# Three of the outer sums of the up product by accumulating DMA, in a two-level Strassen kernel

## The chip, the cores and the metric

The kernel runs on one core of one Trainium2 chip. The metric is the device time of one execution in microseconds (us). A core has five engines that run side by side and meet only at semaphores: PE (TensorE, matrix products), DVE (VectorE) and POOL (GpSimd) for elementwise work, ACT (ScalarE, here copies, scalings and relu), and SP (SyncE, which here only begins transfers). The transfers themselves run on 16 DMA engines that all queues share. In the profile "PEld" is PE's loading of weights, which overlaps its products.

## The reference

Attention without softmax, normalised per head, feeds a mixture of four experts; each token's output is the sum of all four, weighted by given probabilities.

```python
# q, k, v: (8, 8, 576, 64); w1: (4, 512, 1024); w2: (4, 1024, 512); probabilities: (4608, 4)
kv = np.einsum('bhsd,bhse->bhde', k, v)
o = np.einsum('bhsd,bhde->bhse', q, kv)
o = o / np.sqrt(np.mean(o * o, axis=-1, keepdims=True) + 1e-06) * g_norm
x = o.transpose(0, 2, 1, 3).reshape(4608, 512)
p = domain_probs / (domain_probs.sum(-1, keepdims=True) + 1e-09)
for e in range(4):
    h = np.maximum(x @ w1[e], 0.0)           # "up"
    out += p[:, e:e + 1] * (h @ w2[e])       # "down"
```

Everything is float32, inputs and outputs.

## The kernel before

The kernel cuts the 4608 tokens into nine chunks of 512 and works through 36 steps, `s = e * 9 + c`, one for each expert `e` and chunk `c`. A step is an up product (512 tokens by 512 by 1024), relu, and a down product (512 by 1024 by 512).

Both are computed with Strassen's scheme in the Winograd form: seven products of blocks of half the size in place of eight, and more sums. In the up product it is applied twice. The outer level has seven products `m` in the order `OUTER`; each is formed from seven inner products `mm` in the order `ORDER`, whose 128x256 results leave PSUM through ACT copies and DVE additions into one SBUF tile of 128x1024, `made[m]`. The outer sums then combine these seven tiles into the hidden blocks `h[1]`, `h[21]`, `h[4]`, `h[2]` (after relu) and the four differences `h[7]`, `h[5]`, `h[6]`, `h[3]` that the down product needs:

```python
ORDER = (1, 6, 2, 5, 7, 4, 3)
OUTER = (1, 2, 6, 5, 3, 7, 4)
...
def up(s, e, views):
    ...
    def add(key, to, a, b, op=ALU.add, where=either):      # one 128x1024 sum, on DVE or POOL
        combine(key, where(2 * NT), lambda: to.ap[:], lambda: a.ap[:], lambda: b.ap[:], op, [a, b], [to])

    def relu(key, b):
        plan.add(key, act(2 * NT), lambda eng: nc.scalar.activation(
            out=b.ap[:], in_=b.ap[:], func=ACT.Relu), reads=[b], writes=[b])

    for i, m in enumerate(OUTER):
        whole = made[m] = Buf("big", f"m{n}")
        ...                                                 # the seven inner products and their copies
        key = s + (i + 1) / 7
        def unit(f):
            h[f] = Buf("big", f"h{f}_{s}")
            return h[f]
        if m == 2:
            add(key, unit(1), made[1], made[2])
            relu(key, h[1])
        elif m == 6:
            add(key, made[1], made[1], made[6])
        elif m == 5:
            add(key, made[6], made[1], made[5])
        elif m == 3:
            add(key, unit(21), made[6], made[3])
            relu(key, h[21])
            add(key, unit(7), h[1], h[21], ALU.subtract)
        elif m == 7:
            add(key, made[1], made[1], made[7])
            add(key, unit(4), made[1], made[5], where=dve)
            relu(key, h[4])
            add(key, unit(5), h[21], h[4], where=dve)
            add(key, unit(6), h[5], h[1], ALU.subtract, dve)
        elif m == 4:
            add(key, unit(2), made[1], made[4])
            relu(key, h[2])
            add(key, unit(3), h[2], h[6], ALU.subtract)
```

No instruction is written in its final order. Each call of `plan.add` records an operation with the engines that may run it and an assumed cost; `Plan.layout` then plays the program through against those assumptions, and what it settles (which engine, in what order, in which buffer) is the program. So a change of one operation moves many others. The assumptions that matter here are these. In-order engines execute exactly this list, so where a transfer takes longer than assumed, the engine that comes to its result waits, and all that stands behind it waits too.

```python
CROSS, SAME, LANES = 0.3, 0.06, 8             # us from an end to a start on another, the same engine
...
op.end = busy[eng] = t + op.cost[eng]
if op.kb:
    op.end += 5.5                             # a transfer begun on POOL: 5.5 us after its issue
...
def either(n):
    return {"DVE": 0.155 + 0.00104 * n, "POOL": 0.15 + 0.00225 * n}
```

The down product of most steps of the later three experts (`down_deep`) has two levels as well; its inner sums run on DVE or POOL as well. Step 0 uses no Strassen in its up product, and the down products of expert 0 and of each expert's last chunk have one level (`down`). PSUM has eight banks: `u1` and `u2` (two each) for the up products, `db` and `ab` (two each) for the down products and attention. The very last step, 35, is a `down` with nothing after it:

```python
def down(s, e, c):
    ...
    for t in range(2):
        banks = {}
        for j, m in enumerate(MERGED):        # (1, 6, 5, 7, 4, 3, 2)
            kind = "ab" if e and t else "db"
            if m == 1:
                banks[1] = Buf(kind, f"d1_{s}_{t}")
            elif m in (2, 5):
                banks[2] = Buf("u2" if s == E * NCH - 1 else kind, f"d{m}_{s}_{t}")
            ps = banks[1 if m in (1, 6, 7, 4) else 2]
```

The weighted results of the later experts are added to the output in DRAM by transfers begun on POOL with `accum_op=ALU.add` (`send`, line 1065); expert 0 stores plainly from SP. The inputs of each step's up product are loaded again from DRAM by SP into five `xf` buffers.

Of the kernel before, what the change touches and what calls it, by code (L numbers as in the profile page):

```python
# [10 lines left out]
ALU = mybir.AluOpType  # L11
# [23 lines left out]
class Plan:  # L35
# [20 lines left out]
    def add(self, key, cost, fn, reads=(), writes=(), parts=(), kb=0, after=(), port=False, holds=()):  # L56


        op = Op(key, cost, fn, reads, list(writes) + list(parts), kb, port)
        for o in after:  # L60
            op.deps[o] = True
        for b in reads:
            for w in b.writers:
                op.deps[w] = True
            b.readers.append(op)
        for b in writes:
            for o in b.writers + b.readers:
                if o is not op:
                    op.deps[o] = True
            b.readers, b.writers = [], [op]  # L70
        for b in parts:
            b.writers.append(op)
        for b in holds:
            b.readers.append(op)
            op.bufs.append(b)
        for b in op.bufs:
            b.left += 1
        self.ops.append(op)
        return op
# [151 lines left out]
def kernel(  # L231
# [36 lines left out]
    nc = tc.nc  # L268

    B, H, S, D = q.shape  # L270
    E, DM, F = moe_w1.shape
# [5 lines left out]
    NCH = B + 1  # L277
# [56 lines left out]
    plan = Plan()  # L334
# [7 lines left out]
    def act(n):  # L342
        return {"ACT": 0.155 + 0.00088 * n}
# [507 lines left out]
    def up(s, e, views):  # L851
        made = {}
        h = {}

        def add(key, to, a, b, op=ALU.add, where=either):
            combine(
                key, where(2 * NT), lambda: to.ap[:], lambda: a.ap[:], lambda: b.ap[:], op,
                [a, b], [to],
            )

        def relu(key, b):
            plan.add(
                key, act(2 * NT),
                lambda eng: nc.scalar.activation(out=b.ap[:], in_=b.ap[:], func=ACT.Relu),  # L864
                reads=[b], writes=[b],
            )

        for i, m in enumerate(OUTER):
            n = f"{s}_{m}"
            whole = made[m] = Buf("big", f"m{n}")  # L870
            bank = {
                1: Buf("u1", f"u1_{n}"), 2: Buf("u2", f"u2_{n}"), 5: Buf("u2", f"u3_{n}"),
            }
            snap = {}
            for j, mm in enumerate(ORDER):
                key = s + (i + j / 7) / 7
                ps = bank[{2: 2, 5: 5, 3: 5}.get(mm, 1)]

                def product(eng, m=m, mm=mm, ps=ps):
                    for u in range(2):  # L880
                        nc.tensor.matmul(  # L881
                            ps.ap[:, u * P:(u + 1) * P],
                            lhsT=w1f[e][m][mm][1]()[:, u * P:(u + 1) * P], rhs=views[m][mm][1](),
                            start=(mm in (1, 5) and u == 0), stop=True, skip_group_check=True,
                        )

                op = plan.add(
                    key, pe(2, P), product,
                    reads=w1f[e][m][mm][0] + [views[m][mm][0]] + ([ps] if mm == 2 else []),
                    **{"parts" if mm == 2 else "writes": [ps]},  # L890
                    after=last[-2:-1] if mm == 1 else seeds if mm == 5 else (),
                )
                op.marks, op.seed = (ps, HN), mm == 2
                if mm == 3:
                    last.append(op)

                def copy(to, where, ps=ps, key=key):
                    return plan.add(
                        key - 0.4, act(HN),
                        lambda eng: nc.scalar.activation(  # L900
                            out=where(), in_=ps.ap[:, 0:HN], func=ACT.Copy),
                        reads=[ps], parts=[to],
                    )

                def total(a, t, src, add_, whole=whole, key=key):
                    plan.add(
                        key - 0.4, dve(HN),
                        lambda eng: nc.vector.tensor_tensor(  # L908
                            out=block(whole, a, t), in0=src.ap[:, 0:HN], in1=add_.ap[:], op=ALU.add),
                        reads=[src, add_], parts=[whole],  # L910
                    )

                if mm == 1:
                    seeds = [copy(bank[2], lambda b=bank[2]: b.ap[:, 0:HN])]
                elif mm in (6, 7):
                    snap[mm] = Buf("snap", f"s{mm}_{n}")
                    copy(snap[mm], lambda b=snap[mm]: b.ap[:])
                if mm == 2:
                    copy(whole, lambda whole=whole: block(whole, 0, 0))
                elif mm == 7:  # L920
                    total(1, 1, bank[5], snap[7])
                elif mm == 4:
                    copy(whole, lambda whole=whole: block(whole, 1, 0))
                elif mm == 3:
                    total(0, 1, ps, snap[6])
            key = s + (i + 1) / 7

            def unit(f):
                h[f] = Buf("big", f"h{f}_{s}")
                return h[f]  # L930

            if m == 2:
                add(key, unit(1), made[1], made[2])
                relu(key, h[1])
            elif m == 6:
                add(key, made[1], made[1], made[6])
            elif m == 5:
                add(key, made[6], made[1], made[5])
            elif m == 3:
                add(key, unit(21), made[6], made[3])  # L940
# [6 lines that stand above are left out]
                add(key, unit(5), h[21], h[4], where=dve)  # L947
                add(key, unit(6), h[5], h[1], ALU.subtract, dve)
            elif m == 4:
                add(key, unit(2), made[1], made[4])  # L950
                relu(key, h[2])
                add(key, unit(3), h[2], h[6], ALU.subtract)
        hidden[s] = h
# [123 lines left out]
    def down(s, e, c):  # L1077
        h = hidden.pop(s)
        base = s + 1.2
        merge, send = result(s, e, c, base)  # L1080
        second = []
        for t in range(2):
            banks = {}
            for j, m in enumerate(MERGED):
                key = base + (7 * t + j + 0.5) / 14
                kind = "ab" if e and t else "db"
                if m == 1:
                    banks[1] = Buf(kind, f"d1_{s}_{t}")
                elif m in (2, 5):
                    banks[2] = Buf("u2" if s == E * NCH - 1 else kind, f"d{m}_{s}_{t}")  # L1090
                ps = banks[1 if m in (1, 6, 7, 4) else 2]

                def product(eng, m=m, t=t, ps=ps):
                    for kt in range(4):
                        nc.tensor.matmul(  # L1095
                            ps.ap[:, 0:HN], lhsT=four(h[m])[:, kt // 2, t, kt % 2, :],
                            rhs=w2f[e][m].ap[:, kt * HN:(kt + 1) * HN],
                            start=(m in (1, 2, 5) and kt == 0), stop=(kt == 3),
                            skip_group_check=True,
                        )  # L1100

                op = plan.add(
                    key, pe(4, HN), product, reads=[h[m], w2f[e][m]], writes=[ps],
                    after=second[-1:] if t and m in (1, 5) else (),
                )
                op.marks = ps, HN
                if m == 2:
                    second.append(op)
                i, half, fresh = {
                    1: (t, 0, True), 2: (t, 0, False), 6: (t, 1, True), 3: (t, 1, False),  # L1110
                    5: (2 + t, 1, True), 7: (2 + t, 1, False), 4: (2 + t, 0, True),
                }[m]
                merge(key - 0.4, [ps], lambda ps=ps: ps.ap[:, 0:HN], i, half, fresh)
            send(base + 0.5 * (t + 1), t)
            send(base + 0.5 * (t + 1), 2 + t)
# [171 lines left out]
    for e in range(E):  # L1287
        for c in range(NCH):
            s = e * NCH + c
# [14 lines left out]
            if e and c < NCH - 1:  # L1304
                if not primed:
                    banks = [Buf("ab", f"prime{i}") for i in range(2)]
# [20 lines left out]
    with tc.manual_schedule(engines={ENG.PE, ENG.DVE, ENG.Activation, ENG.Pool, ENG.SP}):  # L1327
# [4 lines left out]
        for op in order:  # L1332
# [6 lines left out]
            made = op.fn(op.eng)  # L1339
# [34 lines left out]
```

## Time and profile before

| | |
|---|---|
| time, median of 3 runs | 1730.51 us (1729.95 to 1730.74) |
| span of the profiled execution | 1728.2 us |
| DVE busy | 1224.7 us, 71% |
| ACT busy | 939.3 us, 54% |
| POOL busy | 614.8 us, 36% |
| DMA: SP's queue (q1) / POOL's queue (q0), share of 16 engines | 35.5% / 10.8% |
| accumulating stores, 256 KB, from issue to landing | 5.7 us median |

Busy time is the time in which an engine has an instruction in flight; begun transfers are not counted for the engine that begins them. The share of a queue is the time that its packets took, divided by 16 engines times the span. A group of instructions is named by the line of the kernel, the engine and "out<-in" in the program's names; line 360 is the helper that records every sum, line 864 the relu, line 881 the up product's matrix instructions, lines 1095 and 1170 those of the one-level and the two-level down product, lines 900 and 1198 the ACT copies out of PSUM, line 1065 the accumulating stores. Each float32 product shows as two matrix instructions.

### The profile page before, as it was taken

The numbers are of one execution on the slowest core, as the hardware profiler recorded it, in microseconds if no ns is written. First come the engines' busy times: TensorE is split into PE (matmuls) and PEld (weight loads), VectorE is DVE, ScalarE is ACT, GpSimd is POOL, SyncE is SP. The second block draws the span as 40 slices with busy tenths as digits, with TensorE's granted clock in tenths as the row PEclk, the third lists the DMA queues.
The fourth block names the chain that finished last, engine by engine and source line by source line (L and its number), as shares of the span: only waits on it lengthen the run. The fifth ranks groups of instructions, "written<-read, shape, count | busy, mean of one in ns | idle before, by whom it ended". The sixth has DMA issues, their size and how long they took to land.

```text
span 1728.2 us, 38444 instructions
## 1 busy us (share of the span) xinstructions
PE 1718.7 (99%) x15334; PEld 1651.4 (96%) x15334; DVE 1224.7 (71%) x1969; ACT 939.3 (54%) x2300; POOL 614.8 (36%) x560
## 2 busy tenths in 40 slices
PE   9999999999999999999999999999999999999998
PEld 7699999999999999999999999999999999999998
DVE  4755655565676777777788877777788877777774
ACT  3454544554444565656555556566655566565652
POOL 2421323133334333333345333333345433333331
PEclk9999999999999999999999999999999999999999
DMA  9756444633433353444464344444475344444442
GB/s 236 224 159 193 154 120 131 193 135 128 147 129 100 93 115 103 115 107 113 131 186 110 99 110 111 111 111 110 109 208 112 98 111 111 111 111 103 114 102 49
DMA packets 148596, 220.94 MB, mean 128 GB/s; under 512 B 49600, under 2 KB 90816, under 8 KB 148416
## 3 DMA queue, kind: packets, MB, share of 16 engines
q1 hardware_dynamic: 133312, 191.21, 35.5%
q0 software_dynamic: 15104, 27.27, 10.8%
q8 instruction: 120, 1.97, 0.5%
q14 instruction: 60, 0.49, 0.1%
HBM read 145.30 MB, written 73.14 MB: 126 GB/s over the span
## 4 chain that ended last, share of the span: by engine, by line
PE 99%; POOL 1%; DVE 0%; ACT 0%; issue 0%; POOLq 0%
PE u L881 45%; PE db L1170 19%; PE db L1095 14%; PE ab L1170 12%; PE ab L1095 2%; PE u L968 2%; PE ab L634 1%; PE ab L1323 1%; PE ab L620 1%; PE ab L678 1%; PE ab L660 1%; PE u L1095 1%; POOL rt L551 0%; PE db L660 0%; PE ab L722 0%; PE ab L704 0%
## 5 line engine op out<-in xcount | busy, mean ns | idle before, releaser
L360 DVE TENSOR_TENSOR big<-big,big 128x1024 f32<-128x1024 f32 (+1 forms) x450 | 442.5, 997 | 36.0 <-ACT big L864 23.8
L881 PE MATMUL u<-xf,big 128*128 128x128 f32 x3104 | 453.0, 275 | 0.0
L881 PEld LDWEIGHTS u<-xf,big 128*128 128x128 f32 x3104 | 401.3, 192 | 2.2
L881 PE MATMUL u<-xf,w1y 128*128 128x128 f32 x2652 | 389.6, 275 | 0.0
L908 DVE TENSOR_TENSOR big<-u,snap 128x256 f32<-128x256 f32 x430 | 181.5, 422 | 235.1 <-PE u L881 175.7
L881 PEld LDWEIGHTS u<-xf,w1y 128*128 128x128 f32 x2652 | 343.4, 192 | 2.2
L900 ACT ACTIVATE snap<-u 128x256 f32<-128x256 f32 x490 | 188.1, 384 | 251.3 <-PE u L881 213.9
L1095 PE MATMUL db<-big,big 128*128 128x256 f32 x1120 | 264.1, 380 | 2.1 <-DVE big L560 2.1
L1095 PEld LDWEIGHTS db<-big,big 128*128 128x128 f32 x1120 | 202.9, 190 | 24.6 <-DVE big L560 2.3
L900 ACT ACTIVATE big<-u 128x256 f32<-128x256 f32 x430 | 165.0, 384 | 110.4 <-PE u L881 74.3
L360 POOL TENSOR_TENSOR big<-big,big 128x256 f32<-128x256 f32 (+1 forms) x138 | 170.2, 1241 | 131.6 <-DVE big L360 44.1
L1170 PE MATMUL db<-big,big 128*128 128x128 f32 x1056 | 146.7, 275 | 0.0
L864 ACT ACTIVATE big<-big 128x1024 f32<-128x1024 f32 x128 | 134.4, 1050 | 2.6 <-POOL big L360 1.3
L1170 PEld LDWEIGHTS db<-big,big 128*128 128x128 f32 x1056 | 132.1, 192 | 0.1
L1236 POOL TENSOR_TENSOR big<-big 128x512 f32<-128x512 f32 x26 | 32.9, 1266 | 269.2 <-DVE big L360 263.9
L1198 ACT ACTIVATE snap<-db 128x256 f32<-128x256 f32 x192 | 68.5, 357 | 99.8 <-PE db L1170 94.9
L360 POOL TENSOR_TENSOR big<-big 128x512 f32<-128x512 f32 (+1 forms) x57 | 70.7, 1240 | 126.9 <-DVE big L360 102.6
L1170 PE MATMUL db<-kv,big 128*128 128x128 f32 x804 | 114.6, 275 | 0.0
L1065 POOL DMA_DIRECT2D out_dram<-big x100 | 91.1, 987 | 48.2 <-ACT snap L1198 22.8
L900 ACT ACTIVATE u<-u 128x256 f32<-128x256 f32 x245 | 90.9, 371 | 27.9 <-PE u L881 8.0
L1170 PEld LDWEIGHTS db<-kv,big 128*128 128x128 f32 x804 | 102.1, 192 | 0.1
L1206 DVE TENSOR_TENSOR big<-ab,snap 128x256 f32<-128x256 f32 x140 | 59.2, 423 | 56.7 <-ACT snap L1198 31.9
(218 smaller groups left out, 2686.3 us busy)
## 6 DMA issues: line engine op xcount, KB each, us to landing
xf<-x SPq DMA_DIRECT2D x108, 512.0 KB, 3.6
out_dram<-big POOLq DMA_DIRECT2D x84, 256.0 KB, 5.7
xf<-x_h SPq DMA_DIRECT2D x81, 256.0 KB, 3.0
xf<-x SPq DMA_DIRECT2D x81, 256.0 KB, 3.2
x<-xf SPq DMA_DIRECT2D x36, 512.0 KB, 6.7
big<-in_moe_w_dram SPq DMA_DIRECT2D x25, 512.0 KB, 4.9
small<-in_q_dram SPq DMA_DIRECT2D x72, 128.0 KB, 4.8
kv<-in_k_dram SPq DMA_DIRECT2D x30, 288.0 KB, 5.0
```

Of the source, the lines that this page charges most:

```text
L360: lambda eng: adder(eng).tensor_tensor(out=out_(), in0=a(), in1=b(), op=op),
L864: lambda eng: nc.scalar.activation(out=b.ap[:], in_=b.ap[:], func=ACT.Relu),
L881: nc.tensor.matmul(ps.ap[:, u * P:(u + 1) * P], lhsT=w1f[e][m][mm][1]()[:, u * P:(u + 1) * P], rhs=views[m][mm][1](), start=(mm in (1, 5) ...
L900: lambda eng: nc.scalar.activation(out=where(), in_=ps.ap[:, 0:HN], func=ACT.Copy),
L908: lambda eng: nc.vector.tensor_tensor(out=block(whole, a, t), in0=src.ap[:, 0:HN], in1=add_.ap[:], op=ALU.add),
L968: nc.tensor.matmul(bank.ap[:], lhsT=two(w.ap[:])[:, kt, ut * P:(ut + 1) * P], rhs=two(xh[dh].ap[:])[:, kt, :], start=(dh == kt == 0), stop ...
L1065: nc.gpsimd.dma_start(out=dst, in_=cell(i)[parts, :], accum_op=ALU.add)
L1095: nc.tensor.matmul(ps.ap[:, 0:HN], lhsT=four(h[m])[:, kt // 2, t, kt % 2, :], rhs=w2f[e][m].ap[:, kt * HN:(kt + 1) * HN], start=(m in (1, ...
L1170: nc.tensor.matmul(ps.ap[:, o * P:(o + 1) * P], lhsT=b.ap[:, col:col + P], rhs=w2q[e][m][mm][1]()[:, kt, :], start=(mm in (1, 5) and o == ...
L1198: lambda eng: nc.scalar.activation(out=where(), in_=group_of(ps.ap), func=ACT.Copy),
L1206: lambda eng: nc.vector.tensor_tensor(out=cell(tq, dq), in0=group_of(src.ap), in1=group_of(add_.ap), op=ALU.add,),
L1236: lambda eng: adder(eng).tensor_tensor(out=whole(to), in0=whole(a), in1=whole(b), op=ALU.add),
```

## The change

In the steps 9 to 33 three of the seven outer sums of the up product are no longer instructions of DVE or POOL. POOL begins a transfer from one SBUF tile onto another with `accum_op=ALU.add`, and the DMA engines do the addition in place: `made[2] += made[1]` becomes `h[1]`, `made[6] += made[1]` becomes the next `made[1]`, and `made[4] += made[1]` becomes `h[2]`. Each is 128x1024 float32, 512 KB, and each goes into the plan as 1.0 us of POOL and a landing 5.5 us later. It is meant to take elementwise work off DVE and POOL and to need fewer buffers, since two results are formed in place. The exceptions, expert 0 and the last two steps, keep the instructions.

The kernel before had a change of its own that the changed kernel does not have: in step 35 its second and third result of the down product were put into the `u2` banks, which by then are free. In the changed kernel they are in `db` and `ab` again.

```diff
+        by_dma = e > 0 and s < 34
+
+        def accumulate(key, to, a):
+
+            plan.add(
+                key, {"POOL": 1.0},
+                lambda eng: nc.gpsimd.dma_start(out=to.ap[:], in_=a.ap[:], accum_op=ALU.add),
+                reads=[a, to], writes=[to], kb=512,
+            )
+
...
-            if m == 2:
+            if m == 2 and by_dma:
+                h[1] = made[2]
+                accumulate(key, h[1], made[1])
+                relu(key, h[1])
+            elif m == 2:
                 add(key, unit(1), made[1], made[2])
                 relu(key, h[1])
+            elif m == 6 and by_dma:
+                accumulate(key, made[6], made[1])
+                made[1] = made[6]
+                made[6] = None
             elif m == 6:
                 add(key, made[1], made[1], made[6])
             elif m == 5:
+                made[6] = made[6] or Buf("big", f"v{s}")
                 add(key, made[6], made[1], made[5])
...
             elif m == 4:
-                add(key, unit(2), made[1], made[4])
+                if by_dma:
+                    h[2] = made[4]
+                    accumulate(key, h[2], made[1])
+                else:
+                    add(key, unit(2), made[1], made[4])
                 relu(key, h[2])
                 add(key, unit(3), h[2], h[6], ALU.subtract)
...
                 elif m in (2, 5):
-                    banks[2] = Buf("u2" if s == E * NCH - 1 else kind, f"d{m}_{s}_{t}")
+                    banks[2] = Buf(kind, f"d{m}_{s}_{t}")
```

## The prediction

> **What bounds the kernel now.** I read the page from the top: busy times first, then the chain of waits, and then asked the trace for two stretches of steady steps.
>
> ```profile
> PE 1718.7 (99%) x15334; PEld 1651.4 (96%) x15334; DVE 1224.7 (71%) x1969; ACT 939.3 (54%) x2300; POOL 614.8 (36%) x560
> ...
> PE 99%; POOL 1%; DVE 0%; ACT 0%; issue 0%; POOLq 0%
> PE u L881 45%; PE db L1170 19%; PE db L1095 14%; PE ab L1170 12%; PE ab L1095 2%; PE u L968 2%; PE ab L634 1%; PE ab L1323 1%; PE ab L620 1%; PE ab L678 1%; PE ab L660 1%; PE u L1095 1%; POOL rt L551 0%; PE db L660 0%; PE ab L722 0%; PE ab L704 0%
> ```
>
> 99% of the chain that ended last is PE, and DVE has 0% of it although it is busy 71% of the span. A busy PE need not be PE at its best, since overlapping products hide small gaps. So the next view counts instructions in fixed stretches (columns: stretch, then busy us and count for PE, PEld, DVE, ACT and POOL, the clock granted, the DMA share, GB/s).
>
> ```profile
> 600.00:650.00 50.00, 50.00 (x450) 50.00 (x449) 38.85 (x60) 31.94 (x82) 18.52 (x18) 1.00 0.52 117
> 1500.00:1550.00 50.00, 50.00 (x450) 50.00 (x450) 36.48 (x57) 30.00 (x75) 17.00 (x16) 1.00 0.42 106
> ```
>
> 450 matrix instructions in 50 us, 900 us apart, is one per 111 ns both times, and weight loading is busy for all 50.00 us. The chain at the end of the program shows four in 0.45 us where nothing waits, which is the same pace. So PE has no slack in these steps, at full clock. What PE waits for in the whole program is this (engine, line, what it waited for; total us, times, longest):
>
> ```profile
> PE db L1095 <- DVE big L560: 2.1, 1, 2.1
> PE ab L1323 <- POOL ident masks.py:199: 1.4, 1, 1.4
> PE u L881 <- ACT snap L900: 0.6, 1, 0.6
> PE u L881 <- ACT u L900: 0.5, 1, 0.5
> PE ab L678 <- ACT big L686: 0.4, 1, 0.4
> ```
>
> Five waits, 5.0 us, and the two longest belong to the start and to expert 0's attention, which the change does not touch. **Relief for DVE and POOL is therefore worth next to nothing**: at most the 1.1 us of the two waits at line 881. The change can cost time, though.
>
> **What the Trainium skill says.** "Trainium Kernel Development and Optimization", Best Practices, says to judge TensorE's distance from its roofline by useful work and by how busy weight loading is, not by matmul busy time. This case agrees: 50.00 of 50 us of weight loading in steady steps. "DMA: Bandwidth & Descriptors", Anatomy of one DMA, gives about 2.0 us plus bytes over 436 GB/s for a transfer begun on GpSimd. That makes 3.2 us for 512 KB, an estimate from that page for a plain transfer; the accumulating ones in the trace are slower (256 KB take 3.4 us at best in the window below, where the rule gives 2.6). The same page, Issuing engines are not separate DMA queues, says that transfers from SP and POOL share the 16 DMA engines and interleave. The trace agrees: the spread of landings below is wide. "SBUF — State Buffer", Who interferes with whom, says that a VectorE instruction with two SBUF inputs contends with a GpSimd instruction that reads SBUF. The trace may show it: DVE's sums at line 360 have a median of 1215 ns and reach 3020, though it does not name the cause. It speaks mildly for the change, which takes sums off DVE.
>
> **The change part by part.** *Instructions.* Comparing the built programs, DVE loses 75 sums of 128x1024 (356 become 281), all three sums of 25 steps. It takes over from POOL 16 sums of 128x512, 10 of 128x256 and 6 of the down product's 128x512. With the trace's medians, DVE saves 75 x 1.22 = 92 us and gains about 16 x 0.68 + 10 x 0.41 + 6 x 0.69 = 19, so it is 73 us freer. POOL loses 16 x 1.27 + 10 x 0.73 + 6 x 1.27 = 35 us and gains 75 issues of 0.93 us, which is 69: it is 34 us busier, counted with its issues. PE and ACT do the same work as before. All this lies beside PE, so its direct worth is 0.
>
> *Transfers.* 75 times 512 KB is 39.3 MB on POOL's queue, which has 27.27 MB now. Those take 10.8% of 1728 us, 187 us of all 16 engines, or 1.8 us for each 256 KB. At that rate the new ones take 3.6 us each: 269 us in all, 10.8 us in each step of 44.6. The DMA share of the steady steps would rise from about 0.45 to about 0.69. That is not a bound by itself, but transfers will meet each other more often.
>
> *The new wait.* This decides. A sum on DVE was done 1.22 us after its start. The plan now counts 1.0 + 5.5 + 0.3 = 6.8 us from the issue to the reader's start. The reader of two of the three is a relu on ACT. ACT runs in order, and behind the relu stand the copies that empty the up product's PSUM banks. A transfer that is late holds these up, and PE, which has two banks of a kind, stops soon after. The copies waited for PE 177 times in the later experts, 147.3 us in all, so ACT runs about 0.8 us ahead. I take it that about 0.5 us of lateness is absorbed: trouble starts near 7.3 us from issue to landing. The third sum is read by a sum on DVE or POOL, mostly much later, so I count 50 critical transfers.
>
> How long will one take? The trace has only a relative, 256 KB into DRAM. Columns: count, duration of the issue in ns (minimum, median, maximum), first and last start; then the landing from the issue, first for the whole program and then in one steady step.
>
> ```profile
> L1065 POOL DMA_DIRECT2D out_dram<-big x100: 804/926/1223, 602.7 to 1701.0; - x100
> L1065 POOL DMA_DIRECT2D out_dram<-small x12: 862/877/1213, 777.7 to 1703.9; - x12
> ...
> DMA to landing us min/median/max: 3.0/5.6/8.7
> ```
> ```profile
> L1065 POOL DMA_DIRECT2D out_dram<-big x2: 878/914/950, 1214.8 to 1215.7; - x2
> L1065 POOL DMA_DIRECT2D out_dram<-small x2: 862/870/877, 1225.9 to 1227.1; - x2
> ...
> DMA to landing us min/median/max: 3.4/3.9/7.2
> ```
>
> The fastest takes 3.4 us in that step, the median of all 5.6. The pessimistic end adds the queue's own 1.8 us for the second 256 KB: 5.2 unhindered, 7.4 at the median. The optimistic end adds what plain loads show from 256 KB (3.0 to 3.2 us) to 512 KB (3.6), about 0.5 us: 3.9 and 6.1. SBUF as target may answer faster than DRAM, and these 5.6 include stores begun in pairs, one behind the other. I choose a median near 6.2 us, with one in five of the 50 over 7.3 us by 0.4 us on average: 10 x 0.4 = **4 us**. This is the softest number here.
>
> *The last step.* In the kernel before, the end of the chain reads:
>
> ```profile
> 1697.87 0.45 PE db L1170 x4
> 1698.31 1.73 PE u L1095 x8
> 1700.04 0.89 PE db L1170 x8
> 1700.93 1.91 PE db L1095 x8
> ```
>
> Eight matrix instructions of 256 columns take 1.73 us; the 1.91 hides a wait of 0.18 us for a `db` bank, with 0.45 us of other work in between. So a bank comes back about 0.63 us after the last product into it. At 1698.31 the product in a `u` bank covers exactly such a turn. In the changed program's order nothing stands between those two products into the same `db` bank, so this 0.63 us is paid: **+0.6 us**. The later products alternate between two banks, with 1.73 us for each turn of 0.63, so they need no third.
>
> Sum: 1730.5 + 4 + 0.6 = 1735.
>
> **Rivals.** *The transfers are hidden altogether.* If they land by 6.8 us nearly always, only the tail's 0.6 us is left: about 1731. The 3.4 us and the optimistic end speak for it; the DMA share, already 0.4 to 0.5, speaks against it. *The new wait becomes the bound.* If the addition of SBUF to SBUF is slow, or meets loads often, and the median is 8 us, each of the 50 costs about 0.7 us beyond what is absorbed: +35 us, 1766, and over 2%. The pessimistic end at 7.4 and the maximum of 8.7 speak for it; against it, both pessimistic terms would have to hold together. *The freed DVE speeds the kernel up.* This would need PE waits to remove, and there is 1.1 us of them; best case 1729.5. *Input loads come late, because the DMA engines are busier.* SP's loads of 512 KB land in 3.6 us in the median, into five buffers, while PE uses one for about 44.6 / 7 = 6.4 us. Even twice the landing time is hidden, so I give this 0.
>
> **Range and chances.** Below, PE's fixed work ends the range at 1730. Above, the cost rises steeply with the landing time, so the range is lopsided: a median near 7 us, with half of the 50 late by 0.8 us, gives 20 us, hence 1752. Faster by over 2% would need 35 us, which PE's floor forbids: 0.01. Slower by over 2% needs landings near 8 us: 0.07. Within 2%: 0.92.
>
> **What would show it.** A profile that agrees has PE still at about 450 instructions per 50 us; 75 issues of 512 KB with a median landing of 6 to 6.5 us; DVE busy near 1150 us; POOL's queue near 26% of the 16 engines; and small waits of the relu (ACT, line 874 there) for the new transfers, followed by small waits of PE for ACT. The tail should show a PE wait of 0.6 us for an ACT copy. The prediction is wrong if the median landing is over 7 us or under 5, if POOL's in-order queue delays the issues themselves (an accumulate behind a long sum), or if the new order brings PE waits that no transfer causes.

## The result, and the profile after

The changed kernel takes 1753.13 us (median of 4 runs, 1749.97 to 1755.1) against 1730.51: 1.0129 times as long, 95% interval 1.0112 to 1.0147. That is 22.6 us slower, within 2%, and 1.1 us above the top of my range. The busy times and the chain that ended last, to be held against those of before:

```profile
PE 1728.1 (99%) x15334; PEld 1654.1 (94%) x15334; DVE 1131.6 (65%) x1926; ACT 934.3 (53%) x2300; POOL 645.2 (37%) x603
...
PE 88%; DMA 7%; POOL 2%; ACT 1%; DVE 1%; issue 1%; POOLq 0%; ACTq 0%; DVEq 0%
```

DVE did get freer, by 93 us, and PE still counts as 99% busy. The second line tells more: 7% of the chain is now DMA, where there was none. The two steady stretches, counted again:

```profile
600.00:650.00 50.00, 48.83 (x435) 48.45 (x435) 32.68 (x53) 30.46 (x80) 21.98 (x23) 1.00 0.64 143
1500.00:1550.00 50.00, 49.05 (x437) 48.67 (x436) 32.55 (x54) 30.20 (x78) 21.96 (x23) 1.00 0.64 142
```

435 and 437 matrix instructions in place of 450. Between the starts of PE's weight loads after 515 us (up to the last product), gaps of over 0.26 us sum to 23.7 us beyond the normal pace of 0.11, against 0.4 in the kernel before. That is the loss: 22.4 us of it lie in the steps with sums, 1.3 in the last step. The waits name the way it goes, first PE's and then ACT's:

```profile
PE u L891 <- ACT snap L910: 13.8, 16, 1.8
```
```profile
ACT big L874 <- DMA big<-big: 34.1, 20, 3.4
ACT big L874 <- DMA big<-small: 8.2, 3, 3.1
```

Line 874 is the relu, line 910 the copies out of PSUM behind it, line 891 the up product: the chain that the prediction feared. The view of line 867, where the new transfers are begun, gives their landings:

```profile
L867 POOL DMA_DIRECT2D big<-big x52: 860/880/1182, 521.6 to 1634.4; - x52
L867 POOL DMA_DIRECT2D big<-small x13: 862/874/903, 557.3 to 1605.1; - x13
L867 POOL DMA_DIRECT2D small<-big x10: 870/889/1504, 527.5 to 1427.2; - x10
...
DMA to landing us min/median/max: 4.5/7.4/11.0
```

A fast one takes 4.5 us, comfortably within the plan's 6.8. So why is the median 7.4? The timeline of POOL in one step shows what stands ahead of a slow one (columns: start, duration, what):

```profile
609.22 0.86 POOL L1088 DMA_DIRECT2D out_dram<-big  x1
610.91 0.86 POOL L1088 DMA_DIRECT2D out_dram<-big  x1 [0.83 <-ACT big L1065]
611.89 0.87 POOL L867 DMA_DIRECT2D big<-big  x1
...
616.63 0.89 POOL L867 DMA_DIRECT2D big<-big  x1 [2.29 <-issue]
```

and the chain through the same moment, where it goes:

```profile
610.91 0.86 POOL out_dram L1088
...
611.89 9.21 DMA big<-big
621.10 0.02 issue
621.12 1.06 ACT big L874
...
623.29 1.16 PE u L891 x8
```

Two accumulating stores are begun 2.7 and 1.0 us ahead of the sum of `m = 2`. That sum lands after 9.2 us, ACT's relu starts at 621.12 and PE goes on late. The next sum, of `m = 6` at 616.63, lands after 7.6. Followed back in this way, gap by gap, all but about 1.2 us of the 22.4 end at a late sum of `m = 2`. Taken one by one, the three kinds differ:

| sum | landing, minimum / median / maximum, us | over 7.3 us |
|---|---|---|
| m = 2, right behind two stores in most steps | 4.5 / 8.9 / 10.9 | 21 of 25 |
| m = 6, soon after it | 5.8 / 7.5 / 8.8 | 14 of 25 |
| m = 4, alone in most steps | 4.6 / 5.4 / 8.4 | 3 of 25 |

The packets in the trace show where the time goes. At the issue of each of the 21 late sums of `m = 2`, two to four stores that POOL had begun earlier were still under way; at the other four there was none. With 128 packets counted to each sum in order, a late sum's first packet starts 4.6 us after the issue in the median, against 1.5 us for the other four. In the step above, POOL's queue moves nothing until then but the stores' data, in packets of 2 KB where a sum's have 4 KB. The stores share the engines with loads begun on SP: from 611.9 to 616.3 us POOL's queue took 50.8% of the 16 engines' time and SP's 38.6%.

### The profile page after: what moved, and what is told of

Same layout as the page of the kernel before. It is cut to its first block, busy times and chain, and to the rows that moved or that the text cites. A ratio compares the mean times of both kernels' runs of the same rounds, so it can differ in the third digit from the quotient of the medians.

```text
span 1752.3 us, 38626 instructions
## 1 busy us (share of the span) xinstructions
PE 1728.1 (99%) x15334; PEld 1654.1 (94%) x15334; DVE 1131.6 (65%) x1926; ACT 934.3 (53%) x2300; POOL 645.2 (37%) x603
## 3 DMA queue, kind: packets, MB, share of 16 engines
q1 hardware_dynamic: 133312, 191.21, 35.4%
q0 software_dynamic: 25904, 66.60, 21.9%
## 4 chain that ended last, share of the span: by engine, by line
PE 88%; DMA 7%; POOL 2%; ACT 1%; DVE 1%; issue 1%; POOLq 0%; ACTq 0%; DVEq 0%
PE u L891 39%; PE db L1193 16%; PE db L1118 14%; PE ab L1193 10%; DMA big<-big 5%; PE ab L1118 2%; DMA big<-small 2%; PE u L991 2%; PE ab L634 1%; POOL out_dram L1088 1%; PE ab L678 1%; PE ab L620 1%; PE ab L1346 1%; PE ab L660 1%; DVE big L360 1%
## 5 line engine op out<-in xcount | busy, mean ns | idle before, releaser
L891 PE MATMUL u<-xf,big 128*128 128x128 f32 x3392 | 491.2, 276 | 13.3 <-ACT snap L910 13.3
L891 PEld LDWEIGHTS u<-xf,big 128*128 128x128 f32 x3392 | 436.0, 192 | 19.4 <-ACT snap L910 16.6
L360 DVE TENSOR_TENSOR big<-big,big 128x1024 f32<-128x1024 f32 (+1 forms) x391 | 380.1, 980 | 48.7 <-ACT big L874 28.9
L918 DVE TENSOR_TENSOR big<-u,snap 128x256 f32<-128x256 f32 x446 | 187.9, 421 | 240.9 <-PE u L891 182.3
L360 POOL TENSOR_TENSOR big<-big,big 128x256 f32<-128x256 f32 (+1 forms) x145 | 193.4, 1336 | 219.8 <-DVE big L360 114.2
L910 ACT ACTIVATE big<-u 128x256 f32<-128x256 f32 x446 | 170.7, 383 | 120.4 <-PE u L891 81.5
L1118 PEld LDWEIGHTS db<-big,big 128*128 128x128 f32 x1128 | 205.0, 191 | 25.2 <-DVE big L560 2.3
L1193 PE MATMUL db<-big,big 128*128 128x128 f32 x960 | 134.8, 275 | 0.4 <-ACT snap L1221 0.4
L360 DVE TENSOR_TENSOR big<-big 128x512 f32<-128x512 f32 (+1 forms) x111 | 88.7, 801 | 56.4 <-ACT big L874 55.1
L1193 PEld LDWEIGHTS db<-big,big 128*128 128x128 f32 x960 | 120.7, 192 | 0.6 <-ACT snap L1221 0.6
L360 POOL TENSOR_TENSOR big<-big 128x512 f32<-128x512 f32 (+1 forms) x47 | 60.0, 1277 | 123.6 <-DVE big L360 100.6
```

The lines of the kernel that those rows point to most:

```text
L360: lambda eng: adder(eng).tensor_tensor(out=out_(), in0=a(), in1=b(), op=op),
L891: nc.tensor.matmul(ps.ap[:, u * P:(u + 1) * P], lhsT=w1f[e][m][mm][1]()[:, u * P:(u + 1) * P], rhs=views[m][mm][1](), start=(mm in (1, 5) ...
L910: lambda eng: nc.scalar.activation(out=where(), in_=ps.ap[:, 0:HN], func=ACT.Copy),
L918: lambda eng: nc.vector.tensor_tensor(out=block(whole, a, t), in0=src.ap[:, 0:HN], in1=add_.ap[:], op=ALU.add),
L1118: nc.tensor.matmul(ps.ap[:, 0:HN], lhsT=four(h[m])[:, kt // 2, t, kt % 2, :], rhs=w2f[e][m].ap[:, kt * HN:(kt + 1) * HN], start=(m in (1, ...
L1193: nc.tensor.matmul(ps.ap[:, o * P:(o + 1) * P], lhsT=b.ap[:, col:col + P], rhs=w2q[e][m][mm][1]()[:, kt, :], start=(mm in (1, 5) and o == ...
```

## Experiments

Three theories. **Q**: a sum waits in POOL's queue until the stores ahead of it are through, and the plan, which gives each transfer 5.5 us whatever is in flight, does not know that. **B**: the DMA engines are simply too busy with 39 MB more. **O**: the new order makes PE wait by itself. For the first four runs I had the kinds mixed up: where the recorded text says that `m = 4` stands behind the stores and `m = 2` behind it, the table above has `m = 2` and then `m = 6`. The numbers expected do not depend on the names, except for the landings in the run with half the width. In what follows "slower" is against the kernel before, as run with each experiment (1730.4 to 1730.5 us).

**Stores on another queue.** The addition over the experts is left out.

```diff
-                        nc.gpsimd.dma_start(out=dst, in_=cell(i)[parts, :], accum_op=ALU.add)
+                        nc.sync.dma_start(out=dst, in_=cell(i)[parts, :])
```

> The changed kernel, with the stores of the later experts begun on SP as plain stores at the same places of the program, in place of accumulating ones begun on POOL. The addition over the experts is left out; PE, DVE and ACT keep exactly the changed kernel's order, and the bytes written stay. Theory Q (the sums of m = 4, and behind them those of m = 2, stand in POOL's queue behind two stores of 256 KB begun 1 to 3 us earlier): the landings of the 75 sums fall from a median of 7.4 us to about 5, with hardly one over 7, and the time to 1731.5 to 1733 us. Theory B (the 16 DMA engines are simply too busy, whatever the queue): the bytes are the same, so landings stay over 6.5 us in the median and the time near 1748. Theory O (the new order of the instructions itself makes PE wait): nothing changes, 1753.

Measured: 1731.56 us, ratio 1.0007 (0.9998 to 1.0015). `m = 2` lands after 5.5 us in the median, and of all 75 only one takes over 7.3. PE's waits are again those of the kernel before, plus one in the last step:

```profile
PE db L1118 <- DVE big L560: 2.1, 1, 2.1
PE ab L1346 <- POOL ident masks.py:199: 1.3, 1, 1.3
PE u L891 <- ACT snap L910: 0.6, 1, 0.6
PE u L891 <- ACT u L910: 0.5, 1, 0.5
PE db L1193 <- ACT snap L1221: 0.4, 1, 0.4
```

Theory O falls, since PE, DVE and ACT kept the changed kernel's order exactly. The median of all landings was 6.0 us, not the 5 expected: sharing the engines costs something, but here not time. What SP has begun just before still goes with a late start: in the ten steps where SP had begun a store less than 0.6 us ahead of `m = 2`, its first packet starts 3.0 to 3.6 us after the issue and it lands after 6.8 to 7.7; in the other fifteen it starts by 2.1 and lands after 4.6 to 5.7. One caution: these plain stores also load the engines less, with 84 ns for a packet of 2 KB against 178 for an accumulating one; SP's and POOL's queue took 40.1% and 12.0% of the 16 engines' span, where the changed kernel's took 35.4% and 21.9%. So this run does not tell the other queue from the lighter stores. The run with the stores moved, below, is free of that. This run shows one thing more: 75 sums are off DVE, only one lands late, and nothing is gained.

**The sums as plain copies from SP.** The 75 additions are left out.

```diff
-                lambda eng: nc.gpsimd.dma_start(out=to.ap[:], in_=a.ap[:], accum_op=ALU.add),
+                lambda eng: nc.sync.dma_start(out=to.ap[:], in_=a.ap[:]),
```

> The changed kernel, with its 75 transfers from SBUF to SBUF begun on SP as plain copies in place of accumulating ones begun on POOL; the additions are left out, and PE, DVE and ACT keep the changed kernel's order. The stores stay on POOL's queue. Theory Q: the copies no longer stand behind the stores and land in 3.5 to 4.5 us, in time for the plan's 6.8; the time is 1731 to 1732.5 us. Theory B: 39 MB still cross the same engines beside the stores and loads, so a third of the loss or more stays, 1738 or above. Theory O: 1753.

Measured: 1734.76 us, ratio 1.0027 (1.0018 to 1.0037). It misses Q's number by 2 us and stays below B's. Q's landings fail for `m = 2`: the trace has the landing of 65 of the 75 copies, from 3.2 to 9.3 us, and the 15 over 7.3 are all of `m = 2`, whose median is 7.8. The stores are on the other queue here, yet in the steps that have them `m = 2` lands after 7.1 us or more where the trace has its landing; in the four that have none, 3.2 to 4.6. On SP's queue a load stands ahead of it, begun 0.5 to 1.4 us earlier, in both kinds of step. So another queue alone does not bring `m = 2` in time, and "in POOL's queue" is too narrow: what the runs support is that a sum waits for what has been begun just ahead of it. How much of this is the order within a queue and how much the sharing of the engines, no run separates.

**Half the width.** Each sum covers 512 of its 1024 columns; the rest is left out.

```diff
-                lambda eng: nc.gpsimd.dma_start(out=to.ap[:], in_=a.ap[:], accum_op=ALU.add),
+                lambda eng: nc.gpsimd.dma_start(out=to.ap[:, 0:NT], in_=a.ap[:, 0:NT], accum_op=ALU.add),
```

> The changed kernel, with each of the 75 accumulating transfers cut to its first 512 columns, 256 KB; the addition of the other half is left out and the order of all engines is kept. Theory Q: a transfer of 512 KB took about 3.1 us of its queue, so one behind two stores gains 1.5 us of its own, and one behind another sum gains 3: m = 4 lands near 7.5, m = 2 near 5, and the time is 1732 to 1737 us. Theory B: half of the added traffic goes and about half of the loss, 1740 to 1744. Theory O: 1753.

Measured: 1734.25 us, ratio 1.0023 (1.0014 to 1.0031), within Q's range and not B's. Half of the added bytes remove 5/6 of the loss. `m = 2`, still behind its stores, lands after 7.7 us in the median and `m = 6` after 5.3, where the text, with the names put right, has 7.5 and 5. That costs little: the gaps of the steady steps that are left follow landings of 7.7 to 8.0 us.

**A plan that expects 8.5 us.**

```diff
-                            op.end += 5.5
+                            op.end += 8.5 if op.kb == 512 else 5.5
```

> The changed kernel as it computes, but its scheduler assumes that a 512 KB transfer begun on POOL lands 8.5 us after its issue in place of 5.5, and places all other work by that. Theory Q and the plan's wrong assumption together: landings stay long (median 7 us or more) but nobody waits for them; time 1731 to 1735 us. Theory B: the same, since a late landing is planned for; this run does not tell Q from B. Theory O, or a lack of buffers when tiles are held 3 us longer: 1745 or above.

Measured: 1739.00 us, ratio 1.0052 (1.0037 to 1.0067), outside every range given: 4 us over Q's and B's, 6 under O's. The lateness is planned for: landings still reach 10.9 us, but ACT waits for the new transfers only 2.0 us in all. In their place stands a wait that none of the theories had, at the switch from one expert to the next:

```profile
DVE big L360 <- DMA big<-in_moe_w_dram: 7.9, 3, 5.1
```
```profile
886.22 1.22 PE L891 MATMUL u<-xf,w1y 128*128 128x128 f32 x4 [3.69 <-DVE big L918]
```

DVE stands 5.1 us before a sum of the next expert's weights, whose load is late, and PE, behind DVE, loses about 4 us. The load itself takes 11.7 us from its issue at 872.80, where such loads take about 5 in the median of the changed kernel; from 872 to 884 us the DMA share is 1.03, so the engines had no pause. Whether it was also begun late, because tiles were held 3 us longer, no run separates.

**Which of the sums.** First the two others without `m = 2`, then `m = 2` alone.

```diff
-            if m == 2 and by_dma:
+            if False:
```

> The changed kernel with the first of its three sums (m = 2) an instruction again; m = 6 and m = 4 stay accumulating transfers. (The trace shows, against what I wrote for the first four runs, that the sums which stand behind the stores are those of m = 2, landing at 8 to 10 us, with m = 6 behind them; m = 4 lands near 5.) Theory Q: with m = 2 gone from the queue, m = 6 lands near 5 too, nobody waits, and only the last step's loss of about 1 us stays: 1731 to 1733 us. Theory B: two thirds of the added traffic and so two thirds of the loss stay, 1743 to 1748. The scheduler places everything anew, so a wait that neither theory knows could add some us.

Measured: 1734.78 us, ratio 1.0025 (1.0014 to 1.0036), 2 us over Q's range and far under B's. In the trace no transfer ends a wait of PE in the steady steps. What is left are gaps of 0.81, 0.30, 1.17 and 1.17 us (from start to start) in the last step and single ones at the switches of experts. The two longest of those, 1.06 and 0.39 us, do go back to transfers: ACT stood before a tile until accumulating stores had landed, after 10.1 and 9.5 us.

```diff
-            elif m == 6 and by_dma:
+            elif False:
...
-                if by_dma:
+                if False:
                     h[2] = made[4]
```

> The changed kernel with only the sum of m = 2 as an accumulating transfer, 25 in place of 75; m = 6 and m = 4 are instructions again. Theory Q: in the program's order two stores still stand right ahead of each of them in POOL's queue, so they land at 8 us or later and nearly the whole loss stays, 1744 to 1753 us. Theory B: a third of the traffic and of the loss, 1737 to 1739.

Measured: 1746.67 us, ratio 1.0096 (1.0081 to 1.0111). The time lies in Q's range and not in B's, but not for Q's reason alone. Beyond the normal pace, PE's gaps that go back to a late sum come to 7.4 us here, a third of those in the changed kernel. The rest of the 16.2 us is 2.5 us at a switch, where a DVE sum came late that no transfer had delayed, 2.9 us in the last step, and about 3.4 us (an estimate, half of two stretches of 3.4 us) from a halved clock after two of the gaps, which the last section describes. So the time does not decide between Q and B. The landings do: with a third of the added bytes `m = 2` still lands after 8.4 us in the median, and 19 of 25 take over 7.3.

**The same transfers in another order.** Stores that POOL began less than 3.5 us ahead of a sum, by the plan, are begun right after it. Nothing is left out.

```diff
+        def begins(op, what):
+            return op.eng == "POOL" and op.kb and what in op.fn.__qualname__
...
+        for op in [o for o in order if begins(o, "send")]:
+            at = order.index(op)
+            ahead = [
+                i for i in range(at, len(order))
+                if begins(order[i], "accumulate") and order[i].start - op.start < 3.5
+            ]
+            if ahead:
+                order.insert(ahead[-1], order.pop(at))
...
```

> The changed kernel with all its work and in its order on PE, DVE and ACT; the one difference is that the accumulating stores which POOL began less than 3.5 us ahead of an accumulating sum, by the plan, are begun right after it. Theory Q: m = 2 lands near 5 us in place of 9 and the stores later, which nobody waits for; the time is 1731 to 1733.5 us. Theory B: the same bytes in the same time, 1748 to 1753.

Measured: 1738.07 us, ratio 1.0042 (1.0027 to 1.0056): two thirds of the loss gone with the same bytes and the same sums. The step shown above now reads on POOL, and its `m = 2` lands after 6.4 us in place of 9.2:

```profile
611.88 0.88 POOL L867 DMA_DIRECT2D big<-big  x1 [2.90 <-ACT big L910]
612.48 2.07 POOL L1088 DMA_DIRECT2D out_dram<-big  x2
```

`m = 2` lands after 5.8 us in the median, its first packet starts 1.7 us after the issue, where the late ones of the changed kernel had 4.6, and in the steady steps no gap of PE is left. `m = 6` is still late, 12 of 25 over 7.3 us, and no gap in the steady steps comes of it. This is the run that shows the cause: with the same bytes, what POOL began just ahead of `m = 2` made it late. The miss of some 5 us lies at the switches of experts, where PE has gaps of 7.4 us (without the smallest). Behind them stand these waits of DVE:

```profile
DVE big L360 <- DMA big<-in_moe_w_dram: 6.9, 2, 3.6
DVE big L360 <- DMA out_dram<-big: 4.4, 1, 4.4
DVE small L360 <- DMA out_dram<-small: 3.9, 1, 3.9
```

The last two, worth 4.5 us of PE's gaps, are new: a store begun later holds its tile longer, and DVE was to write that tile. The first, worth 2.9, are loads of the next expert's weights that took 9.3 us; the changed kernel had such waits too, of 3.8 us in all, with a gap of only 0.5 us.

> As the run with the stores begun after the sums, and with the third bank of the last step's down product taken from the u2 pair again, as in the kernel before. Against that run the trace's waits in the last step (0.64, 0.19 and 0.46 us in the changed kernel) should shrink to about the 0.2 us of the kernel before, so the time falls by about 1 us: 1730 to 1732.5, the same as the kernel before. It can't be clearly faster, since PE waited for only 1.1 us in all that these sums could reach.

With the `u2` banks as well: 1736.25 us, ratio 1.0034 (1.0021 to 1.0047). The step in question, 1.8 us, has the right sign; I expected 1. The intervals of the two runs overlap, so the times alone do not show it; the trace does, where the gaps of 0.64 and 0.46 us in the last step are gone. The level is off by the same gaps at the switches.

> As the run with the stores begun after the sums and the u2 banks, but at the switch of experts (the last chunk of one and the first of the next) the stores keep their places, since there a store begun later held a buffer that DVE was to write, and DVE and then PE waited. All sums stay accumulating transfers. The waits of the steady steps stay away; at the switches the changed kernel's own stalls come back, which its trace shows as 4.7 us in all, against 7.4 us there in the run with all stores moved. Expected: 1730.5 plus about 5, 1733 to 1736 us; if the switches are no worse than in the kernel before, 1730 to 1731.

With the stores left in place at the switches: 1733.62 us, ratio 1.0019 (1.0011 to 1.0028), as expected. This is the best version with all three sums by transfer, and it is still slower than the kernel before.

**The last step alone**, on the kernel before:

```diff
-                    banks[2] = Buf("u2" if s == E * NCH - 1 else kind, f"d{m}_{s}_{t}")
+                    banks[2] = Buf(kind, f"d{m}_{s}_{t}")
```

> The kernel before with one part of the change alone: the third bank of the last step's down product comes from db and ab, not from u2. Its order differs in the last step only. From the prediction's step on the tail: one turn of a bank, 0.63 us, is no longer covered, and the changed kernel's trace shows a second uncovered wait of 0.46 us there; expected 0.6 to 1.1 us slower, 1731.1 to 1731.6 us. The rival, that the tail costs nothing since the stores at the end hide it, expects 1730.5.

Measured: 1731.41 us, 0.9 us more than the kernel before as a difference of medians; the interval of the ratio, 0.9998 to 1.0015, has 1 inside it, so the times alone leave it open. The trace is plainer: two new gaps in the last step, 0.64 and 0.46 us, the same as in the changed kernel. The chain shows the first one as PE waiting for a copy:

```profile
1698.62 0.46 PE db L1170 x4
...
1699.10 0.29 ACT snap L1198
...
1699.43 1.16 PE db L1170 x8
```

**The best of the parts**: `m = 6` and `m = 4` by transfer, `m = 2` by instruction, and the `u2` banks.

> The changed kernel with m = 2 an instruction again and the u2 banks of the kernel before in the last step. In the run without m = 2 the trace shows PE stalls of 0.81, 0.30, 1.17 and 1.17 us in the last step and 2.4 us in single waits at the switches of experts, and none that a transfer ends. With the u2 banks the last step should lose about 3 us of stalls: 1731.5 to 1732.5 us, the same as the kernel before within 0.1%. If it is clearly below 1730, taking work off DVE and POOL is worth something after all.

Measured: 1732.03 us, ratio 1.0009 (1.0003 to 1.0016), as expected: 50 sums are off DVE and POOL at a cost of 1.6 us, and at no gain. No version beat the kernel before.

## Why the prediction was wrong

**What bounds the kernel: right.** PE had no slack to give. DVE fell by 93 us (predicted 73) and POOL rose by 30 as the page counts it (predicted 34), and neither brought anything. The run with the stores on SP shows this with all but one of the sums in time.

**The mechanism of the loss: right.** Relu, then the copies, then PE; all three show in the chain. The direction was right too.

**The landing time: the step that failed.** I expected a median near 6.2 us, with ten of the 50 critical transfers over 7.3 us by 0.4 on average. Measured: 7.4, and 24 of the 50 over 7.3 (21 of `m = 2` and 3 of `m = 4`). The unhindered time was not the error: 4.5 us lies inside my bracket of 3.9 to 5.2. The error was to draw the landing as a spread around a median, one transfer like another. It was nearly fixed by what had been begun just ahead: `m = 4`, mostly with nothing ahead of it, 5.4 us, `m = 2` behind its stores 8.9. The built program's order has the two stores right ahead of `m = 2` in step after step; I compared counts in it and did not read what stood ahead of each new transfer. I even wrote that stores begun in pairs land behind one another, and did not carry this over to a sum behind a pair. It was not the load on the engines that I had too low: POOL's queue took 21.9% and not near 26%, since a sum's 128 packets of 328 ns are 2.6 us of 16 engines and not 3.6.

**What is absorbed: too small.** The 21 late sums of `m = 2` landed after 9.1 us on average, 1.8 over my threshold, 37 us together; PE lost about 21 us behind them. With 21 / 21, about 1 us each, trouble starts near 8 us, so about 1.2 us are absorbed and not 0.5. This is an average: four sums of 8.1 to 8.7 us cost PE nothing, one of 8.5 cost it 1 us. The run with half the width agrees: 7.7 us cost little. The two errors partly cancelled, so it is luck that the loss exceeded my range by only 1.1 us.

**The last step: nearly right.** The wait of 0.63 us is there as 0.64. I missed a second of 0.46 among the one-level products, of which I had said that they need no third bank.

**The other rivals.** "The new wait becomes the bound" came in part: transfers are 7% of the chain, and the loss is 22.6 us and not 35. "Hidden altogether" is what the stores on SP make of it. The loads of the inputs (`xf`) end no gap of PE in the changed kernel. The loads of the weights, which I left out, do: 0.5 us there, and more in the runs with the later plan and with the stores moved.

## What to carry to other kernels

Before an instruction is turned into a transfer, read which transfers have been begun just ahead of it at each place, on its own queue first: here the same 512 KB landed after 4.5 us with nothing ahead and after 9 behind two stores. A scheduler that gives each transfer a fixed time cannot see this; it has to keep account of what is under way. Another queue is no sure way out, as the copies on SP's queue show. And where one engine is at its pace all along, taking work off another brings nothing, while a new wait on an in-order engine can cost. Giving that wait more time in the plan, or moving what it collides with, moves other transfers and buffers too; in these runs the next wait then appeared at the switches of experts.

## What the runs showed of the hardware that I had not expected

A stall of PE can cost more than its length, already at 2.6 us (here and below from the start of one weight load to the next). In the run with the later plan, PE stood still for about 4 us until 886.22, and the granted clock went to half at 885.4:

```profile
882.00:884.00 2.00, 0.53 (x5) 0.34 (x4) 0.00 (x0) 0.77 (x2) 0.00 (x0) 1.00 0.89 292
884.00:886.00 2.00, 0.00 (x0) 0.00 (x0) 1.39 (x2) 1.06 (x1) 0.08 (x1) 0.85 0.15 56
886.00:888.00 2.00, 1.78 (x8) 1.78 (x9) 1.63 (x3) 0.00 (x0) 2.00 (x2) 0.50 0.43 144
888.00:890.00 2.00, 2.00 (x11) 2.00 (x11) 0.02 (x1) 0.38 (x1) 2.00 (x2) 0.50 0.34 122
```

Eleven instructions in 2 us in place of eighteen, at a clock of 0.50, for 6.8 us in all. PE worked in 6.0 of these, so an estimate of the extra cost is 3 us. The run with `m = 2` alone had two such drops, of 3.4 us each, which began about 1 us after the end of stalls of 2.6 us. The Trainium skill has this in "TensorE: Matmul & The Clock Gate", Why this matters for your kernels: leave no idle gap of more than about 3 us, since one idle window sends the clock to half. That page's section "What's actually happening" gives the window as 3413 ns; the drops here are one and two of these long. It bit at 2.6 us here, a little earlier than the page says. A stall of 3.1 us in the run with the stores after the sums and the `u2` banks had no drop, and no stall of up to 2.2 us in the steps of the changed kernel had one, so a length alone gives no rule. The same section says that the window runs freely, not tied to the kernel's start; that would fit, but no run here shows it.
